# Batch 0's second softmax part summed beside its products, and nine gate blocks of group 0 split into 384 and 128 columns

## The chip, the cores and the metric

The kernel runs on one core of one Trainium2 chip. The metric is the device time of one execution in microseconds. Five runs of the kernel before took 347.96 to 348.55 us, with a median of 348.24 us. The profile is of one execution, which took 348.22 us; its span, from the first to the last recorded instruction, is 346.4 us.

## What is computed

Sliding-window attention with an ALiBi bias, and then a gated feed-forward layer on its output. Batch is 8, heads are 8, the sequence is 576 long, a head has 64 dimensions; the model width is 512 and the hidden width 1536. Inputs and output are fp32.

```python
scores = scale * np.matmul(q, k.transpose(0, 1, 3, 2))
mask = (rel >= 0) & (rel < 128)                    # rel = query - key
scores = np.where(mask, scores + bias[None], -1e9) # bias = -slope[head] * |rel|
attn = np.exp(scores - scores.max(-1, keepdims=True))
attn = attn / (attn.sum(-1, keepdims=True) + 1e-09)
x = np.matmul(attn, v)              # then heads side by side: 4608 rows of 512
g = x @ w_gate                      # 512 -> 1536
gelu = 0.5 * g * (1.0 + erf(g / sqrt(2)))
out = (gelu * (x @ w_val)) @ w_out  # 1536 -> 512
```

## The kernel before

**Layout.** `xT` holds the attention's result transposed: 128 partitions by four pairs of heads by tokens, in bf16. One pair of heads fills 128 partitions, 64 for each head. The feed-forward layer works on groups of 512 tokens, g = 0 to 8. A batch has 576 tokens, so groups and batches don't coincide. For a group and each of twelve blocks f of 128 hidden columns, `gate_val` makes two chains of four matmuls (over the four pairs), one with `w_gate` and one with `w_val`, each into its own PSUM bank. ScalarE takes the gelu of the first, VectorE multiplies it with the second and writes the tile `hT` (lines 512, 518, 519). `out_part` later multiplies `hT` with `w_out` (line 548).

**PSUM.** There is one pool of eight banks of 128 by 512 fp32. A bank is handed on when the last reader of its earlier content is done. So a matmul that begins a new bank can wait for a gelu, a copy or a multiply of some steps ago.

**Attention of batch 0.** It is done before the loop over groups, in two parts of the queries: 0 to 383 and 384 to 575 (`PARTS`). Keys come in blocks of 64, and each meets the 192 queries that its window can reach; scores lie transposed, keys on partitions, so that `P` (exponentials, bf16) can be used as the moving operand. For queries 0 to 383, `biases0` puts the bias into the bank by a matmul and `scores0` adds the scores; the exponential (line 193) reads the bank. For the rest, `scores0_rest` makes the exponentials without bias, and VectorE multiplies them with `emask` (line 196, `mask`), which holds the bias and the window.

**Sums and inverse of the second part.** `sums4` makes the sums over keys as 32-row results (64 matmuls, line 347), VectorE inverts them (line 352), `spread4` copies each inverse to 64 rows by 16 fp32 matmuls (line 361), ScalarE and VectorE move these to `recip` (line 371), `values` makes the products with v (line 429, 40 matmuls) and VectorE multiplies product and inverse into `xT` (line 484). In `products` the upper and lower 64 rows of the array work at the same time, in 64 by 64 tiles; where the two halves of the keys meet in one bank, a relay through SyncE's queue (line 322) orders them.

Batch 1 has another form, `values_and_sums`: the sums are made by matmuls with a tile of ones (`ones64`) that is 64 columns wide, so that every sum comes out 64 times, on the rows where it is used. They go through `products` with the products with v, and ScalarE inverts them by a logarithm and an exponential.

**Order.** The schedule is manual: each engine executes its instructions in the order in which the code names them. Around the change it is, on TensorE: the scores, first part's sums and products; the spread (`spread_first`, whose multiplies at line 498 write `xT` for tokens 0 to 383); three pairs of heads of `scores0_rest`; block 0 of group 0 in two halves of 192 columns, block 1 on 384; the sums of the second part; block 2 on 384; spread and products of the second part; blocks 0 to 2 on the last 128 columns; blocks 3 to 11 on all 512, with the transposes of batch 1 (line 144) behind blocks 9 and 11. A list `waiting` passed to `gate_val` puts off the gelu and the multiply of a block, so that ScalarE and VectorE meet them later in their order.

**Transfers.** GpSimd issues the loads (lines 102, 127, 134, 735) in the order of the code, eight in flight at most: each waits for the landing of the one eight places before it. The gate weights come in pieces of 128 to 256 hidden columns; columns 512 to 1279 are issued between 14.44 and 18.10 us.

Of the kernel before, what the change touches and what calls it, by code (L numbers as in the profile page):

```python
# [7 lines left out]
FP32 = mybir.dt.float32  # L8
BF16 = mybir.dt.bfloat16
AF = mybir.ActivationFunctionType  # L10
ALU = mybir.AluOpType
# [3 lines left out]
PARTS = (((0, 384), (384, 576)), ((0, 256), (256, 576)))  # L15
# [12 lines left out]
def kernel(  # L28
# [10 lines left out]
    nc = tc.nc  # L39
    B, H, S, D = q.shape  # L40
# [3 lines left out]
    NF = DFF // 128  # L44
# [18 lines left out]
        return psum.tile([128, 512], FP32, name="ps")  # L63


    def keep_busy(ps, n):
        for _ in range(n):
            nc.tensor.matmul(out=ps[:, 0:64], lhsT=zeros, rhs=zeros[:, 0:64], start=True, stop=True)

    wg = consts.tile([128, 4, DFF], BF16, name="wg")  # L70
    wv = consts.tile([128, 4, DFF], BF16, name="wv")
# [1 line left out]
    xT = consts.tile([128, 4, RING], BF16, name="xT")  # L73
# [99 lines left out]
    T = consts.tile([128, H, S], BF16, name="T")  # L173
# [21 lines left out]
    def mask(dst, m):  # L195
        nc.vector.tensor_tensor(out=dst, in0=dst, in1=m, op=ALU.mult)  # L196
# [26 lines left out]
    def biases0(cs, idle=0):  # L223
        pss = []
        for c in cs:
            ps = [bank(), bank()]
            pss.append(ps)
            keep_busy(ps[0], idle)
            for i in (0, 1):
                nc.tensor.matmul(  # L230
                    out=ps[i][:, 0:384].rearrange("p (n x) -> p n x", n=2),
                    lhsT=slopes[:, 2 * c + i, :], rhs=dist.unsqueeze(1).to_broadcast((128, 2, 192)),
                    start=True, stop=False, skip_group_check=True)
                nc.tensor.matmul(
                    out=ps[i][:, 384:512], lhsT=slopes[:, 2 * c + i, :], rhs=dist[:, 0:128],
                    start=False, stop=False, skip_group_check=True)
        return pss

    def scores0(cs, pss):
        for c, ps in zip(cs, pss):  # L240
            for n in range(3):
                for x in (0, 1):
                    q0 = 128 * n + 64 * x
                    w = min(192, 384 - q0)
                    for i in (0, 1):
                        score(0, c, i, 2 * n + x, q0, w,
                              ps[i][64 * x:64 * x + 64, 192 * n:192 * n + w], False)
        for c, ps in zip(cs, pss):
            for i in (0, 1):
                exp(prob(0)[:, c, i, 0:512], ps[i])  # L250
# [238 lines left out]
    def products_first(copies):  # L489
        n = PARTS[0][0][1]  # L490
        for c, ps in enumerate(products(0, [(c, c, 0, n, 0) for c in range(4)])):
            copies[c](out=recip[0][:, c, 0:n], in_=ps[:, 0:n])

    def spread_first():
        _, w = shape(0, 0)
        for g, ps in enumerate(spread4_banks(0, 0)):
            c, x = 2 * (g % 2), g // 2
            nc.vector.tensor_tensor(
                out=xT[:, c:c + 2, w * x:w * x + w], in0=recip[0][:, c:c + 2, w * x:w * x + w],
                in1=ps[:, 0:2 * w].rearrange("p (c x) -> p c x", c=2), op=ALU.mult)  # L500
# [3 lines left out]
    def gate_val(g, f, lo=0, hi=512, later=None):  # L504
        if g not in hid:
            hid[g] = h_pool.tile([128, NF, 512], BF16, name="hT")
        t0 = 512 * g % RING
        n = hi - lo
        pg, pv = bank()[:, 0:n], bank()[:, 0:n]
        for w, ps in ((wg, pg), (wv, pv)):  # L510
            for c in range(4):
                nc.tensor.matmul(  # L512
                    out=ps, lhsT=w[:, c, 128 * f:128 * (f + 1)],
                    rhs=xT[:, c, t0 + lo:t0 + hi], start=(c == 0), stop=(c == 3))

        def act():
            gl = g_pool.tile([128, 512], BF16, name="gelu")
            nc.scalar.activation(out=gl[:, 0:n], in_=pg, func=AF.Gelu)  # L518
            nc.vector.tensor_tensor(out=hid[g][:, f, lo:hi], in0=pv, in1=gl[:, 0:n],  # L519
                                    op=ALU.mult)  # L520

        if later is None:
            act()
        else:
            later.append(act)
# [165 lines left out]
    for t in kT + qT:  # L691
        nc.vector.memset(t[:, :, 576:640], 0.0)
    scores0((1,), biases0((1,)))
    ps0 = biases0((2,))
    second(1, (dve, dve))
    scores0((2, 3), ps0 + biases0((3,)))
    decays(5, 6)
    dve(out=pairs1.rearrange("p x (h d) -> p x h d", d=64),
        in_=vb[1].rearrange("p j x -> p (j x)")[:, 0:1536].rearrange(
# [3 lines left out]
            rest(w, cs, dve)  # L703
    row(0)
    masks = []
    nc.scalar.copy(out=sel8, in_=sel0[:, 0:8:2].unsqueeze(2).to_broadcast((128, 4, 64)))
    sums4(0, 0, lambda: scores0_rest((0,), masks))
    products_first((act, act, act, act))
# [3 lines left out]
    spread_first()  # L712
    decays(6, 8)
    scores0_rest((1,), masks)
    for args in masks:
        mask(*args)
    masks.clear()
    scores0_rest((2, 3), masks)
    masks_of_last_blocks(4, 8)
    for args in masks:  # L720
        mask(*args)
    masks.clear()
    for lo in (0, 192):
        gate_val(0, 0, lo, lo + 192)
    waiting = []
    gate_val(0, 1, 0, 384, waiting)
    sums4(0, 1)
    waiting.pop()()
    gate_val(0, 2, 0, 384)
    spread4(0, 1, (act, dve, act, dve))  # L730
    values(0, 1)
    for f in range(3):
        gate_val(0, f, 384, 512)
    for n in range(2):
        nc.gpsimd.dma_start(
# [25 lines left out]
        return [("table",), 4, ("pv", b - 1), ("s", b, 0, (0,)), 4, ("s", b, 0, (1, 2, 3)), 4,  # L761
                ("s", b, 1, range(4)), ("add", b, 0), ("add", b, 1), 4]

    def flush():
        for args in masks:
            mask(*args)
        masks.clear()


    def exp_table():  # L770
        nc.scalar.preload_act_table_set("natural_log_exp_and_others")
# [4 lines left out]
    for g in range(NG):  # L776
        if 1 <= g < B - 2:
            transposes_dma(3 if g == 1 else g + 2)
        if g == 1:

            nc.gpsimd.tensor_copy(out=mark, in_=qT[1][0:1, 0, 512:514])
            load_qk(4)
            load_v(3)
        for f in range(3 if g == 0 else 0, NF):
            gate_val(g, f)
            if g == 0 and f in (9, 11):
                for c in (0, 1) if f == 9 else (2, 3):
                    for w in (0, 1):
                        transpose(1, w, c, (act, dve)[w])
            if g == 2 and f == 0:  # L790
                add(3, 1)
            if 2 <= g < B - 1:
                if f == (4 if g == 2 else 2):
                    sums4(g + 1, 0)
                    sums4(g + 1, 1)
                if f == (6 if g == 2 else 3):
                    gather(g + 1)
                if f == (8 if g == 2 else 5):
                    spread_dma(g + 1)
                if f == 9 and g + 2 < B:  # L800

                    nc.gpsimd.tensor_copy(out=mark, in_=hid[g][0:1, f, 0:2])  # L802
                    if g + 3 < B:
                        load_qk(g + 3)
                    load_v(g + 2)
        if g == 0:
            nc.gpsimd.memset(Ps[0][:, :, 0:64], 0.0)
            for t in (qs[1], ks[1]):
                nc.gpsimd.memset(t[64:128, 4, :], 0.0)
        for item in steps(g):  # L810
            if isinstance(item, int):
                out_part(g, item)
            else:
                RUN[item[0]](*item[1:])
        store()
        if g == 0:

            nc.gpsimd.tensor_copy(out=mark, in_=kT[0][0:1, 0, 512:514])
            load_qk(3)
            load_v(2)  # L820
# [30 lines left out]
```

## Time and profile before

| what | value |
|---|---|
| median of five runs | 348.24 us (347.96 to 348.55) |
| profiled execution | 348.22 us, span 346.4 us |
| TensorE busy | 338.5 us, 98% of the span |
| VectorE, ScalarE, GpSimd busy | 186.4, 171.6, 107.4 us |
| gate and value matmuls (line 512) | 112.1 and 111.6 us busy |
| output matmuls (line 548) | 96.1 us busy |
| granted TensorE clock | full speed in every slice |

How to read it: a matmul's recorded duration includes the filling of the pipe, and neighbours overlap. The time that a row of matmuls takes is the distance between starts. A remark in square brackets is the idle time of the engine before the row, with what ended it; "issue" is time in which the engine waited for nothing that the profile shows. PE is TensorE, PEld its weight loads, ACT ScalarE, DVE VectorE, POOL GpSimd, SP SyncE. A number such as L512 is a line of the kernel, and a helper's line stands for all its uses. Names in `out<-in` are the program's tiles (`ps` is a PSUM bank, `P` the exponentials, `vb` v, `r` the inverted sums, `rb` the tile `recip`).

### The profile page before, as it was taken

The page shows a single profiled execution, that of the slowest core. Times are in us where ns is not written, and L with a number is a line of the kernel's source. Part 1 is how long each engine was busy: PE and PEld are TensorE (multiplying, and loading weights), DVE is VectorE, ACT ScalarE, POOL GpSimd, SP SyncE. Part 2 cuts the span into 40 slices and gives each one's busy share as a digit, 9 for nine tenths or more (in the row PEclk, how much of TensorE's full clock was granted, in tenths as well). Part 3 has the DMA queues.
Part 4 walks back from the last instruction along what each step waited for, and adds up shares of the span by engine and source line. Part 5 has one row for each costly group of instructions (what it writes and reads, how often), then busy time and mean ns, then how long its engine had stood idle before and what let it go on. Part 6 is the DMA issues. An engine that isn't in the chain of part 4 may idle for free.

```text
span 346.4 us, 8167 instructions
## 1 busy us (share of the span) xinstructions
PE 338.5 (98%) x3368; PEld 170.2 (49%) x3368; DVE 186.4 (54%) x333; ACT 171.6 (50%) x328; POOL 107.4 (31%) x143
## 2 busy tenths in 40 slices
PE   8889999999999999999999999999999999999995
PEld 6665555444544454445544454445444544444443
DVE  6884464434669646953796378635873413303320
ACT  6763488636896337533663447344733133224322
POOL 8865671770590085007700590040000000000000
PEclk9999999999999999999999999999999999999999
DMA  9999999999899399979996899589106120020002
GB/s 174 172 197 190 205 156 172 130 186 169 94 183 194 70 186 182 181 157 94 180 178 147 91 178 189 109 128 112 62 12 128 39 85 0 3 91 30 2 30 91
DMA packets 149705, 43.09 MB, mean 124 GB/s; under 512 B 134532, under 2 KB 142628, under 8 KB 149668
## 3 DMA queue, kind: packets, MB, share of 16 engines
q0 software_dynamic: 108480, 18.49, 70.0%
q1 hardware_dynamic: 37744, 17.70, 21.0%
q10 hardware_dynamic: 3444, 6.38, 8.9%
q8 instruction: 26, 0.43, 0.5%
q14 instruction: 11, 0.09, 0.1%
HBM read 43.65 MB, written 9.53 MB: 154 GB/s over the span
## 4 chain that ended last, share of the span: by engine, by line
PE 88%; ACT 7%; DVE 2%; issue 1%; DMA 1%; ACTq 0%; SPq 0%; DVEq 0%
PE ps L512 54%; PE ps L548 23%; PE ps L429 5%; ACT P L193 5%; PE ps L188 3%; PE ps L347 1%; ACT osb L553 1%; DMA wo<-in_q_dram 1%; DVE osb L553 1%; PE ps L144 1%; PE ps L566 1%; PE ps L361 1%; ACT rb L456 0%; ACT rb L457 0%; PE ps L230 0%
## 5 line engine op out<-in xcount | busy, mean ns | idle before, releaser
L519 DVE TENSOR_TENSOR hT<-ps,gelu 128x512 bf16<-128x512 f32 (+3 forms) x112 | 73.8, 668 | 101.6 <-PE ps L512 91.9
L518 ACT ACTIVATE gelu<-ps 128x512 bf16<-128x512 f32 (+3 forms) x112 | 64.3, 582 | 106.8 <-PE ps L512 98.7
L512 PE MATMUL ps<-xT,wg 128*128 128x512 bf16 (+3 forms) x448 | 112.1, 372 | 0.5 <-DVE xT L484 0.3
L512 PE MATMUL ps<-xT,wv 128*128 128x512 bf16 (+3 forms) x448 | 111.6, 371 | 0.0
L548 PE MATMUL ps<-wo,hT 128*128 128x512 bf16 x420 | 96.1, 380 | 0.0
L512 PEld LDWEIGHTS <-wv 128*128 128x128 bf16 x448 | 43.4, 98 | 50.2 <-issue 0.2
L512 PEld LDWEIGHTS <-wg 128*128 128x128 bf16 x448 | 42.8, 98 | 49.7 <-issue 0.8
L193 ACT ACTIVATE P<-ps 128x384 bf16<-128x384 f32 (+2 forms) x128 | 56.2, 549 | 20.1 <-PE ps L188 19.8
L548 PEld LDWEIGHTS <-hT 128*128 128x128 bf16 x420 | 39.0, 98 | 46.6
L196 DVE TENSOR_TENSOR P<-P,emask 128x768 bf16<-128x768 bf16 (+1 forms) x60 | 34.8, 588 | 20.4 <-ACT P L193 19.6
L102 POOL DMA_DIRECT2D vb<-in_v_dram x40 | 34.0, 903 | 5.2 <-DMA ks<-in_k_dram 1.8
L553 ACT COPY osb<-ps 128x512 f32<-128x512 f32 x25 | 14.7, 589 | 34.2 <-PE ps L548 34.1
L802 POOL COPY mark<-hT 1x2 bf16<-1x2 bf16 x4 | 0.7, 174 | 86.3 <-DVE hT L519 86.3
L102 POOL DMA_DIRECT2D qs<-in_q_dram x30 | 25.2, 860 | 6.5 <-DMA wo<-in_moe_w_out_dram 4.4
L102 POOL DMA_DIRECT2D ks<-in_k_dram x30 | 25.4, 902 | 0.0
L188 PE MATMUL ps<-qT,kT 64*64 64x192 bf16 (+2 forms) x656 | 20.1, 237 | 1.5 <-issue 0.7
L188 PEld LDWEIGHTS <-kT 64*64 64x64 bf16 x656 | 13.2, 107 | 12.1 <-issue 10.0
L484 DVE TENSOR_TENSOR xT<-ps,rb 128x512 bf16<-128x512 f32 (+3 forms) x33 | 15.5, 536 | 6.4 <-PE ps L429 6.4
L429 PE MATMUL ps<-P,vb 64*64 64x192 bf16 (+2 forms) x736 | 17.5, 222 | 0.2
L429 PEld LDWEIGHTS <-vb 64*64 64x64 bf16 x736 | 14.5, 107 | 4.2 <-issue 2.7
L278 DVE TENSOR_TENSOR T<-P 64x1024 bf16<-64x1024 bf16 (+1 forms) x20 | 15.0, 751 | 0.4
L352 DVE RECIPROCAL r<-ps 128x128 f32<-128x128 f32 (+3 forms) x12 | 11.9, 1026 | 0.2 <-PE ps L347 0.2
(82 smaller groups left out, 156.0 us busy)
## 6 DMA issues: line engine op xcount, KB each, us to landing
out_dram<-osb SPq DMA_DIRECT2D x35, 256.0 KB
rb<-rd ACTq DMA_DIRECT2D x10, 576.0 KB
vb<-in_v_dram POOLq DMA_DIRECT2D x32, 128.0 KB, 6.8
qs<-in_q_dram POOLq DMA_DIRECT2D x24, 128.0 KB, 5.2
ks<-in_k_dram POOLq DMA_DIRECT2D x24, 128.0 KB, 6.0
wo<-in_moe_w_out_dram POOLq DMA_DIRECT2D x2, 768.0 KB, 14.7
wg<-in_moe_w_gate_dram POOLq DMA_DIRECT2D x5, 256.0 KB, 8.1
wv<-in_moe_w_val_dram POOLq DMA_DIRECT2D x5, 256.0 KB, 8.7
```

Source lines behind the costliest of these rows:

```text
L102: nc.gpsimd.dma_start(out=t[0:n, j, :].rearrange("p (h d) -> p h d", h=H), in_=src[b][:, 128 * j:128 * j + n, :].rearrange("h p d -> p h d"))
L188: nc.tensor.matmul(out=out, lhsT=keys(b, c, m)[half, :], rhs=qT[b % 2][half, c, q0:q0 + n], start=first, stop=True, skip_group_check=not f ...
L193: nc.scalar.activation(out=dst, in_=src, func=AF.Exp, scale=0.125)
L196: nc.vector.tensor_tensor(out=dst, in0=dst, in1=m, op=ALU.mult)
L278: nc.vector.tensor_tensor(out=to[half, :, 2 * n0 + x:2 * n1 + x - 1:2], in0=P[half, :, 3 * n0:3 * n1 - 2:3], in1=P[half, :, 3 * n0 + 1:3 * ...
L429: mm = nc.tensor.matmul(out=out, lhsT=lhsT, rhs=prob(b)[half, c, i, col:col + q1 - q0], start=all(t[2] != u for t in todo[:n]), stop=True, ...
L484: nc.vector.tensor_tensor(out=xT[:, c, at:at + e - a], in0=src, in1=recip[b][:, c, a:e], op=ALU.mult)
L512: nc.tensor.matmul(out=ps, lhsT=w[:, c, 128 * f:128 * (f + 1)], rhs=xT[:, c, t0 + lo:t0 + hi], start=(c == 0), stop=(c == 3))
L518: nc.scalar.activation(out=gl[:, 0:n], in_=pg, func=AF.Gelu)
L519: nc.vector.tensor_tensor(out=hid[g][:, f, lo:hi], in0=pv, in1=gl[:, 0:n], op=ALU.mult)
L548: nc.tensor.matmul(out=acc[g], lhsT=hid[g][:, f, 128 * t:128 * (t + 1)], rhs=wo[:, f, :], start=(f == 0), stop=(f == NF - 1))
L553: (nc.vector.tensor_copy if g < B - 2 and t in by_dve.get(g, (0, 2)) else nc.scalar.copy)(out=osb, in_=acc[g])
```

## The change

Four things change, all in group 0 and batch 0.

- The transposes of k for the pairs 2 and 3 (`second(1, ...)`) come before the bias matmuls of pair 2, and pairs 2 and 3 are done one after the other.
- Block 0's first half (tokens 0 to 191) runs between the scores of pair 1 and those of pairs 2 and 3; both its halves put off gelu and multiply until ScalarE is past the exponentials.
- The second part's sums are made by `products` in the form of batch 1, with `ones64`, in one sequence with the products with v (`products_rest`): 20 and 40 matmuls. VectorE inverts the four banks' halves in four reciprocals of 192 columns, spread between the multiplies of blocks 1 to 5 (`inverse_rest`). Their results are put in the unused tile `T`, read as fp32. ScalarE copies the products from PSUM to `recip` in two copies, and one multiply of VectorE (`scale_rest`) writes `xT`. `sums4`, `spread4` and `values` of that part fall away.
- Blocks 2 to 8 run on columns 0 to 383 first, and then blocks 0 to 8 on the last 128. The loop over groups begins at block 9 for group 0.

`keep_busy` has a width as an argument that nothing here uses, and `flush` moves up in the file.

```diff
+    lo0 = PARTS[0][1][0]
+    inverse = T.rearrange("p h x -> p (h x)").bitcast(FP32)[:, 0:4 * (S - lo0)].rearrange(
+        "p (c x) -> p c x", c=4)
+
+    def products_rest():
+        w = S - lo0
+        pss = products(0, [(n, slice(2 * n, 2 * n + 2), lo0, S, 0) for n in (0, 1)] + [
+            (2 + c // 2, c, lo0, S, w * (c % 2)) for c in range(4)])
+        for n in (0, 1):
+            nc.scalar.copy(out=recip[0][:, 2 * n:2 * n + 2, lo0:S],
+                           in_=pss[2 + n][:, 0:2 * w].rearrange("p (c x) -> p c x", c=2))
+        return pss
+
+    def inverse_rest(c, pss):
+        w = S - lo0
+        nc.vector.reciprocal(inverse[:, c, :], pss[c // 2][:, w * (c % 2):w * (c % 2) + w])
+
+    def scale_rest():
+        nc.vector.tensor_tensor(out=xT[:, :, lo0:S], in0=recip[0][:, :, lo0:S], in1=inverse, op=ALU.mult)
...
     scores0((1,), biases0((1,)))
-    ps0 = biases0((2,))
     second(1, (dve, dve))
-    scores0((2, 3), ps0 + biases0((3,)))
+    for c in (2, 3):
+        scores0((c,), biases0((c,)))
...
     scores0_rest((1,), masks)
-    for args in masks:
-        mask(*args)
-    masks.clear()
+    flush()
+    waiting = []
+    gate_val(0, 0, 0, 192, waiting)
     scores0_rest((2, 3), masks)
     masks_of_last_blocks(4, 8)
-    for args in masks:
-        mask(*args)
-    masks.clear()
-    for lo in (0, 192):
-        gate_val(0, 0, lo, lo + 192)
-    waiting = []
+    flush()
+    gate_val(0, 0, 192, 384, waiting)
+    for later in waiting:
+        later()
+    waiting.clear()
     gate_val(0, 1, 0, 384, waiting)
-    sums4(0, 1)
+    pss = products_rest()
+    inverse_rest(0, pss)
     waiting.pop()()
-    gate_val(0, 2, 0, 384)
-    spread4(0, 1, (act, dve, act, dve))
-    values(0, 1)
-    for f in range(3):
+    for f in range(2, 9):
+        gate_val(0, f, 0, 384)
+        if f < 5:
+            inverse_rest(f - 1, pss)
+        if f == 5:
+            scale_rest()
+    for f in range(9):
         gate_val(0, f, 384, 512)
...
-        for f in range(3 if g == 0 else 0, NF):
+        for f in range(9 if g == 0 else 0, NF):
```

More of the change, by code (lines that the diff above doesn't have):

```diff
@@ L63, in bank, with keep_busy @@
         return psum.tile([128, 512], FP32, name="ps")
-    def keep_busy(ps, n):
+    def keep_busy(ps, n, w=64):
         for _ in range(n):
-            nc.tensor.matmul(out=ps[:, 0:64], lhsT=zeros, rhs=zeros[:, 0:64], start=True, stop=True)
+            nc.tensor.matmul(out=ps[:, 0:w], lhsT=zeros, rhs=zeros[:, 0:w], start=True, stop=True)
     wg = consts.tile([128, 4, DFF], BF16, name="wg")
@@ L705, with flush @@
     masks = []
+    def flush():
+        for args in masks:
+            mask(*args)
+        masks.clear()
     nc.scalar.copy(out=sel8, in_=sel0[:, 0:8:2].unsqueeze(2).to_broadcast((128, 4, 64)))
@@ L762, in steps @@
                 ("s", b, 1, range(4)), ("add", b, 0), ("add", b, 1), 4]
[L764 to L767, printed above, removed]
     def exp_table():
```

## The prediction

> **What bounds the kernel now.** I read the page's first part, then the chain that ended last, then the order of time of each engine between 8 and 46 us, the only stretch that the edit touches.
>
> ```profile
> PE 338.5 (98%) x3368; PEld 170.2 (49%) x3368; DVE 186.4 (54%) x333; ACT 171.6 (50%) x328; POOL 107.4 (31%) x143
> ...
> PE 88%; ACT 7%; DVE 2%; issue 1%; DMA 1%; ACTq 0%; SPq 0%; DVEq 0%
> ```
>
> TensorE is busy for 98% of the span and is 88% of the chain. A microsecond taken off its queue, in work or in waiting, is a microsecond off the end, as long as nothing else becomes late. From 28 us on it hardly waits, so all is won or lost before that.
>
> ```profile
> 18.25 0.47 PE L188 MATMUL ps<-qT,kT 64*64 64x192 bf16 x17 [0.75 <-issue]
> 18.65 0.50 PE L512 MATMUL ps<-xT,wg 128*128 128x192 bf16 x4
> ...
> 19.98 0.81 PE L512 MATMUL ps<-xT,wg 128*128 128x384 bf16 x4
> 20.63 0.81 PE L512 MATMUL ps<-xT,wv 128*128 128x384 bf16 x4
> 21.37 1.03 PE L347 MATMUL ps<-P,ones 64*32 64x64 bf16 x64
> 22.34 0.82 PE L512 MATMUL ps<-xT,wg 128*128 128x384 bf16 x4
> 23.00 0.81 PE L512 MATMUL ps<-xT,wv 128*128 128x384 bf16 x4
> 23.74 0.93 PE L361 MATMUL ps<-r,sel 32*128 32x96 f32 x16
> 24.60 0.96 PE L429 MATMUL ps<-P,vb 64*64 64x64 bf16 x40
> 25.91 1.01 PE L512 MATMUL ps<-xT,wg 128*128 128x128 bf16 x4 [0.34 <-DVE xT L484]
> 26.75 0.38 PE L512 MATMUL ps<-xT,wv 128*128 128x128 bf16 x4
> 26.97 0.39 PE L512 MATMUL ps<-xT,wg 128*128 128x128 bf16 x4
> ...
> 27.87 1.03 PE L512 MATMUL ps<-xT,wg 128*128 128x512 bf16 x4
> ```
>
> This is TensorE in order of time (start, duration, matmuls). Durations overlap, so I take costs from one start to the next. Four matmuls cost 0.65 us on 384 columns (19.98 to 20.63), 0.22 us on 128 (26.75 to 26.97), 0.864 us on 512 (27.87 to 28.73): 163, 56 and 216 ns each. The second part of batch 0 is seen whole: 64 sums (L347), 16 spread matmuls in fp32 (L361), 40 products (L429), then a hole, since the gates of the last 128 columns wait for xT piece by piece.
>
> ```profile
> 11.14 2.06 ACT L193 ACTIVATE P<-ps 128x512 bf16<-128x512 f32 x4 [0.98 <-PE ps L188]
> ...
> 18.58 1.64 ACT L193 ACTIVATE P<-ps 128x384 bf16<-128x384 f32 x4 [0.19 <-PE ps L188]
> 20.23 1.28 ACT L518 ACT_TABLE_LOAD   x1
> 21.53 0.94 ACT L518 ACTIVATE gelu<-ps 128x192 bf16<-128x192 f32 x3
> ```
>
> ScalarE: at 11.14 it had stood idle 0.98 us for the scores of heads 4 and 5. From 18.58 it is full: exponentials, table, gelus.
>
> ```profile
> 14.56 1.36 DVE L352 RECIPROCAL r<-ps 128x192 f32<-128x192 f32 x1 [0.21 <-PE ps L347]
> ...
> 17.99 1.01 DVE L498 TENSOR_TENSOR xT<-rb,ps 128x384 bf16<-128x384 f32 x2
> ...
> 20.45 1.03 DVE L196 TENSOR_TENSOR P<-P,emask 128x768 bf16<-128x768 bf16 x2
> ```
>
> VectorE: one reciprocal of 192 columns, 1.36 us; the xT products of the first part, which end at 17.60, 18.06, 18.53 and 19.00; the last masks, done at 21.48.
>
> **The change, part by part.** Times are on the clock of before; part 1's shift comes on top.
>
> 1. *Transposes of k moved ahead of a bias (8.9 to 13.2 us).* The 12 transposes start right behind the scores that begin at 8.62, at 8.95, not at 9.51 (their k landed at 8.55: issued at 2.25, 6.3 us to landing). They take 0.47 us. VectorE's copy of pair 2 then waits for its memsets, done at 9.59, and starts at 9.60, not 10.07. Scores and the exponentials at 11.14 follow 0.47 earlier, and the copy at L698 at 10.62, not 11.01 (its transfer landed at 10.4). As ScalarE's four exponentials end at 12.7 instead of 13.2, the sums behind them, the reciprocal, the spread and xT all move. Value: -0.45. If k lands late or a copy is held: 0; a loss is excluded, as the moved work is the same.
>
> 2. *First gate block split around the scores.* Its first half (8 matmuls on 192 columns, 0.083 us each) now needs only the first two xT products. Two go at 17.72; six wait for 18.06 + 0.12 (18.53 to 18.65 is that delay in the trace) and end at 18.68. 24 scores at 0.024 us: 19.26; 8 gates: 19.93. Before: 19.98. Value: -0.05. The 0.75 us gap put down to issue falls at the twentieth matmul from 16.93. There TensorE is now held by xT until past 18.25, so it costs nothing; were it to come again elsewhere, +0.75.
> The price is on ScalarE: scores 4 and 5 end at 18.97, 0.2 us later their exponentials start (19.17, not 18.58), 1.64 us, table 1.28 us: the two gelus end at 22.44 and 22.66, some 0.6 us later than before.
>
> 3. *Sums beside the products.* Removed from f1's end (21.28) to f3's start (27.87), 6.59 us: all but f2 (1.30) and three blocks of 128 (1.34), so 3.95 us: sums, spread, products 2.7 and waits 1.2. Added: 60 matmuls (20 sums, 40 products). In the built program they wait for the last mask (21.5), run ten sums, then wait for the banks of the two halves of block 0, so for both gelus: 22.72. The 46 left at 0.022 us are 1.03. That per-matmul cost is the second part of batch 1, which has the same shape (102 matmuls, 57.46 to 59.71); the first part there gives 0.032, so +0.45 as the high end. With 0.1 for the change of tiling f2 starts at 23.85: 2.62 us from f1's end at 21.23, against 3.95. Value: -1.33. Behind these waits stand f2 and all gates.
>
> 4. *384, then 128 columns.* Six more blocks are split: 6 x 8 x (163 + 56 - 216 ns) = +0.13 us. f2 to f8 run from 23.85 to 32.98, the nine narrow blocks take 72 x 56 ns = 4.0 us.
> Here a rule speaks against the change. The Trainium skill ("TensorE: Matmul & The Clock Gate", section "Back-to-back issue gap") gives 81 ns as the sustained spacing of 128-column matmuls that each load weights, and 56 ns only for the isolated gap. By it the narrow blocks cost 72 x 25 ns = 1.8 us more and the sum turns to about +0.1. The row here has weights loaded for each, and 20 of them from 26.75 to 27.87 keep 56 ns; the same rule's 131 ns for 512 columns is 216 here. I take the row.
>
> 5. *VectorE in place of the spread.* Four reciprocals of 192 columns (1.36 each) and one scaling, among the multiplies of f1 to f5 (0.53), under f2 to f8's 9.1 us of TensorE. No row shows a scaling of 768 columns from two fp32 tiles in SBUF. The rows of 192, 384 and 512 columns (346, 548, 690 ns) give 140 + 1.075 per column: 0.97 us; the Trainium skill ("VectorE: DVE Perf Modes", section "Mode 2×_2P — use both read ports for one tensor") holds fp32 tensor_tensor at 1×, at 0.96 GHz 0.80 us plus a fixed part, an estimate. I take 0.97. Queue: first reciprocal at 23.5, two copies on ScalarE, f1's gelu to 25.1, multiplies of f1 and f2 to 26.4, then three reciprocals, three multiplies, scaling: done near 32.7. TensorE asks for it at 32.98. Cover: 0.3 us; each tenth that a reciprocal is longer takes 0.4 of it. Banks and gelu buffers come free over 0.4 us ahead.
>
> 6. *Transfers.* Weights are wanted earlier: f8 at 31.7, not 36.5.
>
> ```profile
> wv<-in_moe_w_val_dram POOLq DMA_DIRECT2D x1, 256.0 KB, 10.0
> ```
>
> That is its transfer, issued at 18.10, landed at 28.1. GpSimd's queue is unchanged but for its memset of T, which now waits for the scaling; it ran at 36.68, so nothing moves. The transfer for f10 landed at 37.06, wanted near 40. All stay hidden.
>
> Sum: -0.45 - 0.05 - 1.33 + 0.13 = -1.70 us. The profiled execution took 348.22 us (span 346.4 and 1.8 around it): 346.5. The median of the runs is 348.24, so the two can be compared.
>
> **Rivals.**
> - *Part 1 gives nothing* (k's landing at 8.55 or the memsets hold it): 346.95. For it: 0.05 us between landing and need.
> - *VectorE becomes the bound*: at 1.6 us a reciprocal the scaling ends 1.0 later, 0.7 past its cover: 347.2; with the sums at 0.032 us a matmul 347.7. Against: the row at L352 has the same shape.
> - *Narrow blocks at 81 ns*, at the nine blocks: 348.3, slower than before by 0.1. It decides from 79 ns; from 90 ns it is measurably slower. Against: the 20 matmuls above.
> - *The gain is lost later*, since a transfer holds batch 1 (its v landed at 49.2, first used at 53.4): 348.2. Against: TensorE's list of waits names nothing over 0.1 us behind 27 us.
> - *The gelus hold less than I think* (TensorE finds its banks at once): another 0.7 off, 345.8.
>
> **How the numbers follow.** Forecast 0.55 (own range 346.1 to 347.0), part 1 empty 0.13, VectorE 0.14, narrow blocks 0.06, lost later 0.07, fewer waits 0.05. Leaving out the narrow blocks, the loss and the worst of VectorE gives 345.8 to 347.6. 0.2% (0.70 us) is about what a measurement can tell from no change. Faster: 0.55 + 0.13 + 0.12 + 0.05 = 0.85. Of the rest 0.10 stays within the bound and 0.05 is slower.
>
> **What would show it.** Part 1: four exponentials from about 10.7. Part 2: TensorE held near 17.9, not at "issue". Part 3: L361 with 16 matmuls, not 32; in the second part a wait for a gelu of 0.5 to 0.9 us, then 46 matmuls in about 1 us. Part 4: 128-column matmuls at 56 ns over nine blocks, and f9 1.7 us earlier than 38.23. Part 5: the scaling ends before the first narrow block. I am wrong if TensorE waits for xT there, if narrow blocks pass 60 ns, or if f9 comes early and the end doesn't.

## The result, and the profile after

The changed kernel takes 346.72 us (median of 22 runs, 346.19 to 348.43); the kernel before takes 348.26 us beside it (43 runs). The ratio is 0.9943, with a 95% interval of 0.9929 to 0.9957: faster by 1.5 us. The profiled execution took 347.24 us (span 345.4), half a microsecond more than the median, and what was late in it is seen below. In many runs, of the kernel before too, TensorE's granted clock fell to half for some microseconds (a mean clock of about 0.99 over the run), and the medians of such runs lie 0.6 to 2.3 us above those of the others; so where it matters I give beside the median of all runs, as "at full clock", that of the runs with a mean clock of at least 0.998: for the changed kernel 21 of 23 (with the profiled one), at 346.71.

The first part of the page of the changed kernel, and its chain that ended last:

```profile
PE 336.7 (97%) x3356; PEld 171.5 (50%) x3356; DVE 189.8 (55%) x337; ACT 172.8 (50%) x334; POOL 107.5 (31%) x143
...
PE 86%; ACT 7%; DMA 2%; DVE 2%; issue 1%; POOL 1%; POOLq 0%; ACTq 0%; DVEq 0%
```

TensorE lost 1.8 us of work (338.5 before), though the span fell by 1.0 only: DMA has gone from 1% to 2% of the chain. TensorE in order of time shows where (start, duration, matmuls, and in brackets the idle time before and what ended it):

```profile
10.18 0.41 PE L188 MATMUL ps<-qT,kT 64*64 64x192 bf16 x12 [0.21 <-DVE kT L152]
...
12.54 0.60 PE L682 MATMUL ps<-ident,wo 64*128 64x64 bf16 x24 [1.06 <-DVE wo L720]
...
16.52 0.93 PE L361 MATMUL ps<-r,sel 32*128 32x192 f32 x16 [0.40 <-ACT rb L492]
17.38 0.36 PE L188 MATMUL ps<-qT,kT 64*64 64x128 bf16 x12
18.21 0.70 PE L534 MATMUL ps<-xT,wg 128*128 128x192 bf16 x4 [0.47 <-ACT emask L639]
...
20.30 0.81 PE L534 MATMUL ps<-xT,wg 128*128 128x384 bf16 x4
20.95 0.81 PE L534 MATMUL ps<-xT,wv 128*128 128x384 bf16 x4
21.70 0.70 PE L429 MATMUL ps<-P,ones 64*64 64x128 bf16 x10
22.91 0.65 PE L429 MATMUL ps<-P,vb 64*64 64x128 bf16 x17 [0.51 <-ACT gelu L540]
...
24.12 0.82 PE L534 MATMUL ps<-xT,wg 128*128 128x384 bf16 x4
```

The kernel before had, on TensorE and then on VectorE:

```profile
12.01 0.60 PE L660 MATMUL ps<-ident,wo 64*128 64x64 bf16 x24 [0.45 <-DVE wo L698]
...
16.93 0.57 PE L188 MATMUL ps<-qT,kT 64*64 64x128 bf16 x19
```

```profile
11.01 0.94 DVE L698 COPY wo<-vb 128x1536 bf16<-128x1536 bf16 x1
```

From above: the scores of pair 2 come early (part 1), but the transposes at 12.54 wait 1.06 us and are 0.53 *later* than before. So the scores of pair 1's second part start at 17.38 instead of 16.93. The row at 18.21, the first half of block 0, waits 0.47 us; it names ScalarE's `emask`, which ended at 18.09, but the first tile of xT that it needs was done at 18.06 (VectorE's L520), and the traces of six variants put the same wait down to xT. From there on the change wins: f1 ends at 21.60, ten sums run, TensorE waits for the gelus, and f2 starts at 24.12. The blocks that follow, up to f9:

```profile
32.58 0.81 PE L534 MATMUL ps<-xT,wv 128*128 128x384 bf16 x4
33.23 0.39 PE L534 MATMUL ps<-xT,wg 128*128 128x128 bf16 x4
...
37.25 1.03 PE L534 MATMUL ps<-xT,wg 128*128 128x512 bf16 x4
```

Seven blocks on 384 columns take 9.11 us, 163 ns a matmul; nine on 128 take 4.02 us, 72 matmuls at 55.8 ns. f9 starts at 37.25, not 38.23. From f9 to the end both spans have 308.2 us, so nothing is given back later.

ScalarE and VectorE of the same execution:

```profile
10.64 2.06 ACT L193 ACTIVATE P<-ps 128x512 bf16<-128x512 f32 x4 [0.53 <-PE ps L188]
...
19.58 1.64 ACT L193 ACTIVATE P<-ps 128x384 bf16<-128x384 f32 x4 [0.73 <-PE ps L188]
21.23 1.28 ACT L540 ACT_TABLE_LOAD   x1
22.53 0.55 ACT L540 ACTIVATE gelu<-ps 128x192 bf16<-128x192 f32 x2
```

```profile
11.53 0.95 DVE L720 COPY wo<-vb 128x1536 bf16<-128x1536 bf16 x1 [0.94 <-DMA vb<-in_k_dram]
...
23.88 1.36 DVE L511 RECIPROCAL T<-ps 128x192 f32<-128x192 f32 x1 [0.37 <-PE ps L429]
...
31.40 0.94 DVE L514 TENSOR_TENSOR xT<-rb,T 128x768 bf16<-128x768 f32 x1
```

The four exponentials start at 10.64, not 11.14, as part 1 meant. But VectorE's copy from vb stood idle for 0.94 us until k's rows had landed, and ran at 11.53. The scaling ended at 32.34, and the narrow blocks wanted it at 33.23.

In this execution the steps add up to: +0.45 at 17.38, -0.13 from there to the end of block 0 (part 2: f1 starts 0.32 later, not 0.45), -1.43 from f1's end to f2 (2.52 us against 3.95), +0.13 for the narrow blocks: -0.98, which is the shift of f9.

### The profile page after: what moved, and what is told of

Its sections match the earlier page's. It is cut to its first block, busy times and chain, and to the rows that moved or that the text cites. A ratio compares the mean times of both kernels' runs of the same rounds, so it can differ in the third digit from the quotient of the medians.

```text
span 345.4 us, 8164 instructions
## 1 busy us (share of the span) xinstructions
PE 336.7 (97%) x3356; PEld 171.5 (50%) x3356; DVE 189.8 (55%) x337; ACT 172.8 (50%) x334; POOL 107.5 (31%) x143
## 4 chain that ended last, share of the span: by engine, by line
PE 86%; ACT 7%; DMA 2%; DVE 2%; issue 1%; POOL 1%; POOLq 0%; ACTq 0%; DVEq 0%
PE ps L534 54%; PE ps L570 23%; PE ps L429 5%; ACT P L193 4%; DMA vb<-in_k_dram 2%; PE ps L188 2%; PE ps L347 1%; ACT osb L575 1%; DVE osb L575 1%; PE ps L588 1%; PE ps L144 1%; ACT rb L456 0%; ACT rb L457 0%; ACT L540 0%; PE ps L361 0%
## 5 line engine op out<-in xcount | busy, mean ns | idle before, releaser
L540 ACT ACTIVATE gelu<-ps 128x512 bf16<-128x512 f32 (+3 forms) x118 | 65.3, 561 | 103.2 <-PE ps L534 97.1
L534 PEld LDWEIGHTS <-wv 128*128 128x128 bf16 x472 | 45.0, 98 | 48.8
L534 PEld LDWEIGHTS <-wg 128*128 128x128 bf16 x472 | 44.3, 98 | 48.6 <-issue 0.9
L196 DVE TENSOR_TENSOR P<-P,emask 128x768 bf16<-128x768 bf16 (+1 forms) x60 | 34.8, 588 | 20.5 <-ACT P L193 19.6
L484 DVE TENSOR_TENSOR xT<-ps,rb 128x512 bf16<-128x512 f32 (+3 forms) x29 | 14.3, 562 | 6.3 <-PE ps L429 6.3
L352 DVE RECIPROCAL r<-ps 128x128 f32<-128x128 f32 (+2 forms) x11 | 11.1, 1050 | 0.1
```

Source lines behind the costliest of these rows:

```text
L484: nc.vector.tensor_tensor(out=xT[:, c, at:at + e - a], in0=src, in1=recip[b][:, c, a:e], op=ALU.mult)
L534: nc.tensor.matmul(out=ps, lhsT=w[:, c, 128 * f:128 * (f + 1)], rhs=xT[:, c, t0 + lo:t0 + hi], start=(c == 0), stop=(c == 3))
```

## The experiments

My theory was the forecast: each part gives what its step says. Its rival after this trace: the transfer into vb holds part 1 in any case. The first four kernels ask that; the next four take the other parts one by one; the last four follow what these showed. The groups ran on different chips, each beside the kernel before.

### Part 1: alone, undone, and with no transfer to wait for

The kernel before with part 1 alone:

```diff
-    ps0 = biases0((2,))
     second(1, (dve, dve))
-    scores0((2, 3), ps0 + biases0((3,)))
+    for c in (2, 3):
+        scores0((c,), biases0((c,)))
```

> The kernel before, with part 1 alone (the transposes of k ahead of the two biases). Step 1 of the forecast: 0.45 us less, 347.8 us, the four exponentials from about 10.7 and the 24 transposes (ps from wo) from about 11.6 instead of 12.01. Rival, read from the trace of after: the copy into wo waits for the transfer of k's runs into vb, which lands about when the copy was due before; then the exponentials move to 10.7 but the transposes stay at 12.0 or later, and the median stays at 348.1 to 348.3.

Measured: 348.38 us (14 runs), before 348.52 beside it, ratio 1.0005 (0.9978 to 1.0031); at full clock 348.24 and 348.37. Part 1 alone gives about a tenth of a microsecond or nothing. The interval of the ratio, -0.8 to +1.1 us, could not tell 0.45 from nothing; the runs at full clock just can (-0.13, with a 95% interval of -0.37 to 0.14 when these runs are resampled). The changed kernel with the same lines put back:

```diff
+    ps0 = biases0((2,))
     second(1, (dve, dve))
-    for c in (2, 3):
-        scores0((c,), biases0((c,)))
+    scores0((2, 3), ps0 + biases0((3,)))
```

> The changed kernel with part 1 undone. Step 1 of the forecast: 0.45 us more than the changed kernel's median of 346.72, so 347.15. Rival (the transfer holds the copy in any case): 346.7 to 346.85.

Measured: 346.97 (22 runs), at full clock 346.76 against the changed kernel's 346.71. That is 0.05 more at full clock (-0.15 to 0.41 by the same resampling) and 0.25 over all runs. By the ratios to the kernel before, 0.9955 (0.9941 to 0.9969) and 0.9943, it is 0.4, but their intervals overlap. At full clock both experiments leave out step 1's 0.45, though the second does so narrowly, and the traces show where it goes. The transfer is a part of the reason, and not the whole of it. This is VectorE, and then TensorE, with part 1 alone:

```profile
10.30 0.95 DVE L698 COPY wo<-vb 128x1536 bf16<-128x1536 bf16 x1 [0.40 <-DMA vb<-in_k_dram]
```

```profile
11.31 0.60 PE L660 MATMUL ps<-ident,wo 64*128 64x64 bf16 x24 [0.52 <-DVE wo L698]
...
16.22 0.57 PE L188 MATMUL ps<-qT,kT 64*64 64x128 bf16 x19
18.54 0.47 PE L188 MATMUL ps<-qT,kT 64*64 64x192 bf16 x17 [1.75 <-issue]
```

In this execution TensorE's scores of pair 1 ran at 7.87, before at 8.62, so all had a head start of 0.75 us; 0.66 of it was there at the first scores (5.84, before 6.50), ahead of the place of the edit. Part 1 added its 0.45 to that up to the exponentials, and the copy, held by the transfer for 0.40, gave it back: the scores of 16.22 are 0.71 ahead of before's 16.93, the head start alone. Then comes what I had not looked for. TensorE stopped at the twentieth of these matmuls, at the same place as before, for 1.75 us instead of 0.75, and resumed at 18.54, before at 18.25. The gap put down to "issue" took the whole head start; I conclude that it would have taken part 1's gain with it.

The two other kernels take the transfer's landing out, by letting the copy read rows that landed long before. The scores of batch 0's columns from 384 on are then made from other rows, by the same instructions:

```diff
     dve(out=pairs1.rearrange("p x (h d) -> p x h d", d=64),
-        in_=vb[1].rearrange("p j x -> p (j x)")[:, 0:1536].rearrange(
+        in_=qs[0].rearrange("p j x -> p (j x)")[:, 0:1536].rearrange(
```

In the changed kernel:

> The changed kernel, but the copy into wo reads from qs, which has landed by 8 us, in place of vb: batch 0's scores of the columns from 384 on are made from the wrong rows, with the same instructions and the same transfers. If the transfer into vb is what held part 1's gain: the copy starts at about 10.6, the transposes from 11.6, f9 near 36.3, and the median falls by 0.3 to 0.5 from 346.72, to 346.2 to 346.4, with a narrower spread of the runs (the profiled run within 0.2 of the median). If the transfer held it in the profiled run alone: median 346.65 to 346.75.

In the kernel before:

> The kernel before with the same edit (the copy into wo reads qs; batch 0's scores of the columns from 384 on are made from the wrong rows). In its trace the copy ran at 11.01 when VectorE came to it, with the transfer landed at 10.4: if that is its usual state, nothing changes: 348.15 to 348.3. If the transfer holds before's copy too in most runs: 347.9 or less. Under either, runs above 349.5 become rare if they are late landings of this transfer, and stay if they are something else.

Measured: 346.99 (9 runs; at full clock 346.96), and 348.66 (14 runs; 348.48 at full clock, before 348.37). Nothing was gained by either; at full clock the first was 0.25 slower than the changed kernel. This is TensorE of the first of the two:

```profile
16.32 0.36 PE L188 MATMUL ps<-qT,kT 64*64 64x128 bf16 x12
17.27 0.69 PE L534 MATMUL ps<-xT,wg 128*128 128x192 bf16 x4 [0.59 <-DVE xT L520]
...
19.11 0.33 PE L534 MATMUL ps<-xT,wv 128*128 128x192 bf16 x2 [0.97 <-issue]
```

Here part 1 gave all that step 1 promised: its copy ran at 10.40 without a wait, and from the scores of pair 1 (8.46) to those of 16.32 are 7.86 us, in the kernel before 8.31. And yet the third of wv's matmuls waited 0.97 us at the gap, to 19.11, with part 2 in place. The transfer takes part 1's gain in some executions (the copy waited for it 0.15 to 0.94 us in five of the eight traces that have both part 1 and this wait), and where it doesn't, the gap does.

### What the gap is

The page's list of DMA queues has two of kind "instruction". The larger, q8, has 26 packets, 0.43 MB, so about 16 KB each; the transfer view by windows shows when each starts. With part 1 alone, 16.00 to 17.00 us:

```profile
q0 software_dynamic: 458, 0.18, 146.6%
q8 instruction: 1, 0.02, 6.8%
```

One such packet starts in that stretch, among 458 of the loads, and takes about 1.1 us (6.8% of the time of sixteen DMA engines). In the kernel before the same packet starts at 15.89. Set against TensorE's gaps:

| kernel | TensorE ready | packet starts | TensorE resumes | resume - packet |
|---|---|---|---|---|
| before | 17.50 | 15.89 | 18.25 | 2.36 |
| part 1 alone | 16.79 | 16.06 | 18.54 | 2.48 |
| before, no transfer | 16.80 | 15.82 | 18.27 | 2.45 |
| split alone (below) | 17.43 | 15.87 | 18.23 | 2.36 |
| changed, no transfer | 18.14 | 16.79 | 19.11 | 2.32 |
| changed, no part 2 (below) | 16.79 | 15.74 | 17.99 | 2.25 |
| changed, f2 first (below) | 18.07 | 15.93 | 18.33 | 2.40 |
| changed, short cover (below) | 18.28 | 16.12 | 18.55 | 2.43 |

"Ready" is the end of the matmuls before the gap, and varies by 1.5 us; "resumes" follows the packet, at 2.25 to 2.48 us. The packet takes about 1 us of that; what fills the rest the profile does not show. In the changed kernel's own trace the packet started at 15.87, so by the same distance its instructions were there at about 18.2, and TensorE, late by the transfer and held until 18.21, did not meet the gap.

In three of these traces (part 1 alone, f2 first, short cover) there is a first gap of the same sort, of 0.17 to 0.30 us, at the last of the first 32 sums (L347). Between it and the second gap lie, with f2 first, 1 + 12 + 32 + 48 + 16 + 12 + 4 + 2 = 127 matmuls, each with a weight load: 254 instructions, and a few waits. The Trainium skill ("Runtime: NRT & Kernel Launch", section "Instruction fetch mechanics") says that an engine's instruction memory is refilled in blocks of 16 KiB, 256 instructions, through a DMA queue of its own; packet size and spacing agree, and roughly the number: the changed kernel's 3356 matmuls and as many weight loads are 6712 instructions, 26.2 blocks, which is why I take q8 for TensorE's queue. It also calls the crossing of a block "mostly hidden": here it was not. It cost 0.17 to 1.75 us, in a stretch in which all DMA engines were busy with loads and TensorE ran short instructions.

To test it, I made TensorE's stream shorter without changing its work in time: the warm-up at the start as 32 matmuls on 128 columns, not 64 on 64.

```diff
-    keep_busy(held[0], 64)
+    keep_busy(held[0], 32, 128)
```

> The changed kernel with the warm-up at the start made of 32 matmuls on 128 columns in place of 64 on 64: the same TensorE time, 32 matmuls (64 instructions with their weight loads) fewer in TensorE's stream. In the traces so far the gap put down to issue stands at the same place of the stream (two gaps 127 matmuls apart, 256 instructions with the waits between), and it ends 2.3 to 2.45 us after the second 16 KB packet of the instruction queue starts, whenever TensorE arrived. If the block of instructions arrives by its own time: the gap's place moves 32 matmuls later, behind the scores of pairs 2 and 3, where TensorE comes after 19 us, no gap is left before 20 us, and the median falls from 346.71 by the 0.26 to 0.97 us of the gaps in the traces of its variants, less what the wait for xT takes over: 346.2 to 346.5. If the block is fetched when TensorE asks for it, the gap moves along and keeps its size: 346.7.

Measured: 348.84 (22 runs), 347.50 in its four runs at full clock: slower than the changed kernel, so my expectation was wrong. But the trace shows where the gap belongs:

```profile
12.78 0.46 PE L347 MATMUL ps<-P,ones 64*32 64x128 bf16 x19
14.96 0.47 PE L347 MATMUL ps<-P,ones 64*32 64x64 bf16 x13 [1.71 <-issue]
```

The first gap now stands 32 matmuls further down: from the last of the first 32 sums, past 12 scores, to the twentieth of the second 32. The first packet started at 12.79 instead of 10.18 to 10.45 (the eleven kernels with the old warm-up; 12.2 and 12.3 in the two other runs with the short one), and TensorE resumed 2.17 us later. So the gap belongs to a place in the stream, a block's boundary, and the packet is not on a fixed timetable: with the stream 64 instructions shorter, TensorE reaches the boundary later, and the packet came later too. The same with part 1 undone:

> The same with part 1 undone. If the instruction block was what swallowed part 1's gain, part 1 is worth its 0.45 us once the block is out of the way: 0.3 to 0.45 above the run with part 1 and the short warm-up, with scores (1) starting near 16.9 to 17.2 here and near 16.3 there. If part 1 is empty for another reason, the two agree within 0.1.

Measured: 348.90 (22 runs; six at full clock, 347.69). That doesn't tell part 1's worth with the block out of the way, as the block wasn't out of the way:

```profile
14.70 0.47 PE L347 MATMUL ps<-P,ones 64*32 64x64 bf16 x13 [1.04 <-issue]
```

TensorE was ready at 13.66 and resumed at 14.70; with part 1 it was ready 0.41 earlier, at 13.25, and resumed at 14.96. It came earlier and waited longer, by 0.67.

What makes a packet start when it does is not settled. In all fourteen traces the second packet of the stretch starts 5.4 to 6.4 us after the first, however early TensorE was; a chain in which a block is asked for after the one before has come would look like that. I have no run that shows it.

### Part 4 alone

The kernel before, with its own sums, spread and products, but f3 to f8 on 384 columns and then nine blocks on 128:

```diff
     values(0, 1)
-    for f in range(3):
+    for f in range(3, 9):
+        gate_val(0, f, 0, 384)
+    for f in range(9):
         gate_val(0, f, 384, 512)
...
-        for f in range(3 if g == 0 else 0, NF):
+        for f in range(9 if g == 0 else 0, NF):
```

> The kernel before, with part 4 alone: f3 to f8 on 384 columns behind the old sums, spread and products, then nine blocks on 128. Step 4: six more blocks split cost +0.13; the wait of 0.34 us for xT ahead of the first narrow block, which the blocks on 384 now cover, goes, and the narrow blocks all run at 56 ns: 348.0 to 348.1. By the 81 ns rule: 72 x 25 ns more, 349.9.

Measured: 347.76 (21 runs), before 348.49, ratio 0.9964 (0.9947 to 0.9980); at full clock 347.56 and 348.27. That is 0.7 us faster, where I expected 0.15 to 0.25. The trace:

```profile
24.57 0.96 PE L429 MATMUL ps<-P,vb 64*64 64x64 bf16 x40
25.47 0.82 PE L512 MATMUL ps<-xT,wg 128*128 128x384 bf16 x4
...
33.28 0.39 PE L512 MATMUL ps<-xT,wg 128*128 128x128 bf16 x4
...
37.30 1.03 PE L512 MATMUL ps<-xT,wg 128*128 128x512 bf16 x4
```

A gate starts at 25.47, 0.90 after the products began. In the kernel before the first narrow block began at 25.91 and its second half at 26.75, since its matmuls waited piece by piece for xT: from 25.50, 0.90 behind the start of its products, the first 8 narrow matmuls took until 26.97: 1.47 us, for 0.45 of work. So the hole behind the products was 1.02 us, not the 0.34 that the bracket names ahead of it. It is gone, less 0.13 for the split: -0.89, and f9 is at 37.30, against 38.23, 0.93 earlier. The 72 narrow matmuls take 4.02 us, 55.8 ns each, here too, and not the 81 ns that step 4 of the forecast quotes.

### The cover of VectorE's work

The changed kernel with f2 to f5 only ahead of the narrow blocks, and f6 to f11 on 512 columns:

```diff
-    for f in range(2, 9):
+    for f in range(2, 6):
...
-    for f in range(9):
+    for f in range(6):
         gate_val(0, f, 384, 512)
...
-        for f in range(9 if g == 0 else 0, NF):
+        for f in range(6 if g == 0 else 0, NF):
```

> The changed kernel with only f2 to f5 on 384 columns ahead of the narrow blocks (f0 to f5), f6 on at 512. By step 5 the cover is TensorE's work on blocks f2 to f8: without three of them the narrow blocks start at 24.12 + 4 x 1.30 = 29.3 but the scaling ends near 31.9, so TensorE waits about 2.5 us for xT: about 2.4 us slower than the changed kernel, 349.1, and slower than before. If VectorE's chain could be done much earlier than it was: 346.7.

Measured: 350.94 (18 runs), 349.45 at full clock; 2.7 us slower than the changed kernel, and slower than before (ratio 1.0060, 1.0044 to 1.0076). TensorE, and below it VectorE:

```profile
32.05 0.40 PE L534 MATMUL ps<-xT,wg 128*128 128x128 bf16 x4 [2.92 <-DVE xT L514]
```

```profile
23.52 1.36 DVE L511 RECIPROCAL T<-ps 128x192 f32<-128x192 f32 x1 [0.37 <-PE ps L429]
...
31.05 0.95 DVE L514 TENSOR_TENSOR xT<-rb,T 128x768 bf16<-128x768 f32 x1
```

From the first reciprocal to the end of the scaling are 8.5 us, and TensorE waits for them. Part 4's blocks ahead of the narrow ones are what makes part 3's inverse on VectorE free: with three fewer it costs 2.7 us. Part 3 with no block of part 4 was not run.

### Part 2 undone, and f2 ahead of the products

```diff
-    gate_val(0, 0, 0, 192, waiting)
     scores0_rest((2, 3), masks)
     masks_of_last_blocks(4, 8)
     flush()
-    gate_val(0, 0, 192, 384, waiting)
-    for later in waiting:
-        later()
-    waiting.clear()
+    for lo in (0, 192):
+        gate_val(0, 0, lo, lo + 192)
```

> The changed kernel with part 2 undone: scores of pairs 2 and 3 first, then both halves of gate block 0. By the price in step 2, the exponentials start about 0.6 us earlier, so do table load and gelus, and the wait for the gelus inside the products shrinks from 0.5 by up to that: 346.2 us. Rival: the gap of 0.75 us put down to issue, which part 2 hid, comes back behind 17 us: 346.7 to 347.0.

Measured: 346.36 (5 runs, 345.93 to 346.54), ratio to before 0.9934 (0.9910 to 0.9958), against the changed kernel's 0.9943: 0.35 less on the medians, though the intervals overlap. The trace says why, and that both expectations held a part of it:

```profile
17.99 0.47 PE L188 MATMUL ps<-qT,kT 64*64 64x192 bf16 x17 [1.20 <-issue]
...
21.11 0.53 PE L429 MATMUL ps<-P,ones 64*64 64x128 bf16 x10
21.65 0.65 PE L429 MATMUL ps<-P,vb 64*64 64x128 bf16 x17
...
22.85 0.82 PE L534 MATMUL ps<-xT,wg 128*128 128x384 bf16 x4
```

The gap is back, 1.20 us. But the scores of pairs 2 and 3 are out at 18.4, not 19.6, the gelus end at 21.8, and from the end of f1 (21.02) to f2 there are 1.83 us instead of 2.52. What part 2 hid at the gap in the changed kernel's trace it paid at the gelus. With five runs and intervals that overlap, the 0.35 itself is not shown beyond the noise.

f2's 384 columns ahead of the sums, to fill the wait for the gelus:

```diff
+    gate_val(0, 2, 0, 384, waiting)
     pss = products_rest()
     inverse_rest(0, pss)
-    waiting.pop()()
+    for later in waiting:
+        later()
     for f in range(2, 9):
-        gate_val(0, f, 0, 384)
+        if f > 2:
+            gate_val(0, f, 0, 384)
```

> The changed kernel with block f2's 384 columns run ahead of the sums and products. If TensorE's hole between the first ten sums and the seventeen products (about 1.0 us in the trace of after, from 21.95 to 22.91) is only the wait for the banks that the gelus hold, f2 fills it, and f3 starts about 24.4 instead of 25.43: 0.6 to 1.0 us less, 345.7 to 346.1, the lower gain if the scaling (then some 0.3 later, wanted 1.0 earlier) makes the narrow blocks wait. If the products need something else that is late (masks, a mode change), the hole moves behind f2 and the time stays at 346.6 to 346.8.

Measured: 346.41 (5 runs), ratio 0.9937 (0.9913 to 0.9961), 0.3 less:

```profile
21.67 0.81 PE L534 MATMUL ps<-xT,wv 128*128 128x384 bf16 x4
22.41 0.55 PE L429 MATMUL ps<-P,ones 64*64 64x128 bf16 x10
...
24.53 0.81 PE L534 MATMUL ps<-xT,wg 128*128 128x384 bf16 x4 [0.50 <-ACT rb L505]
```

The products now run without a wait, but 0.50 us is lost behind them: f3 needs a bank, and the copies of the products (L505) stand on ScalarE ahead of f1's gelu. So I put the gelus ahead and took the two edits together, with the scaling behind f4's multiply. First, with the short warm-up as well:

```diff
-    gate_val(0, 1, 0, 384, waiting)
+    gate_val(0, 1, 0, 384)
+    gate_val(0, 2, 0, 384)
     pss = products_rest()
     inverse_rest(0, pss)
-    waiting.pop()()
-    for f in range(2, 9):
+    for f in range(3, 9):
         gate_val(0, f, 0, 384)
-        if f < 5:
-            inverse_rest(f - 1, pss)
-        if f == 5:
+        if f == 3:
+            inverse_rest(1, pss)
+        if f == 4:
+            inverse_rest(2, pss)
+            inverse_rest(3, pss)
             scale_rest()
```

> The changed kernel with the short warm-up, without part 2, with f2 ahead of the products, f1's and f2's gelus ahead of the copies of the products, and the scaling behind f4's multiply. From the trace without part 2 (f2 at 22.86, gap of 1.20): without the gap f1 ends about 0.7 earlier, f2 fills what is left of the wait for the gelus, and the products follow: f3 near 22.9 instead of 24.2, f9 near 34.9 to 35.3; 344.6 to 345.3 us. If the gap stays, 345.8 or more; if the scaling becomes late, TensorE waits for xT ahead of the narrow blocks and the time is 345.5 to 346.2.

Measured: 347.66 (13 runs), none at full clock: its trace has the early gap, 1.35 us, and half the clock from 14.2 to 21.0. With the old warm-up:

> The changed kernel with the old warm-up, without part 2, with f2 ahead of the products, f1's and f2's gelus ahead of the copies, the scaling behind f4's multiply. The gap put down to issue stays (16.8 to about 18.0, ended 2.4 us after the instruction packet of 15.8), so f1 ends near 21.1 as in the run without part 2; f2 then fills to 22.4, the products run without a wait for 1.34 us, and f3 starts near 23.75 instead of 24.16: 0.4 less than that run's 346.36, 345.8 to 346.1. If the gains of the run without part 2 and of the run with f2 first are one and the same wait, the two don't add and it stays at 346.3 to 346.45.

Measured: 346.96 (22 runs), 346.08 in its 11 runs at full clock, ratio to before 0.9951 (0.9932 to 0.9970). In its trace the products take 1.26 us and nothing waits; the gap stays (0.80 us, to 18.21), and f3 started at 23.90, where I had 23.75:

```profile
22.64 0.46 PE L429 MATMUL ps<-P,ones 64*64 64x128 bf16 x10
...
23.90 0.82 PE L534 MATMUL ps<-xT,wg 128*128 128x384 bf16 x4
```

At full clock this is the fastest of these kernels, by 0.3 over the two single edits and 0.6 over the changed kernel; over all runs it is not, because half of them have the clock drop. No version here beats the changed kernel beyond the intervals.

## Why the prediction was right, and where it wasn't

The forecast was 346.5, the median is 346.72, within the likeliest case's own range of 346.1 to 347.0. The sum was -1.70 us; the medians give -1.54. That the number held took some luck: step 1's 0.45 did not come, which alone makes 346.97 of the forecast, just inside the range; in the trace steps 2 and 3 gave 0.18 more than forecast, and about 0.1 between that sum (-1.43) and the medians is not accounted for. Of the signs named, "f9 1.7 us earlier" did not show in the profiled execution (0.98); the others did, nearly as written.

- *Step 1, -0.45: failed.* The transposes and exponentials moved as it said (10.64). The step that failed is "the sums behind them, the reciprocal, the spread and xT all move. Value: -0.45". In five of eight traces they didn't in full, as the copy then waited for k's rows in vb, which I had dated from one execution; where they did, TensorE waited longer at the block's boundary. The medians: -0.14 alone, 0.05 to 0.25 when undone. The rival "part 1 gives nothing" is what happened, though not for the reasons that it names (the landing of the k that is transposed, the memsets). The step's own "or a copy is held: 0" covers the first half of it; the gap behind it was not in the forecast for this step.
- *Step 2, -0.05.* In the trace it was -0.13. I had seen the gap of 0.75 and said that it "costs nothing" once TensorE is held by xT. That held in the changed kernel's own trace; in three others with part 2 the gap still cost 0.97, 0.26 and 0.27 us (no transfer, f2 first, short cover). I didn't ask what the gap was, nor apply it to step 1, upstream of the same place: a wait that doesn't end sooner when TensorE comes sooner takes in whatever is gained before it. The price on ScalarE was seen ("some 0.6 us later"), but booked in step 3. Undone, part 2 looks like a loss of about 0.35, on five runs.
- *Step 3, -1.33.* In the trace -1.43: 2.52 us from f1's end to f2, where I had 2.62; the wait ended 1.31 us behind f1, where I had 1.49, and the matmuls after it took 1.21 us to f2, where I had 1.13. Part of that is a slip: behind ten of 60 matmuls 50 are left, as in the trace, not 46. The total was right and its owner wrong. I booked "waits 1.2" among what the sums beside the products remove. The split alone removes 1.02 of them, with the old sums in place. What is left for the merged sums and VectorE's inverse is -1.43 + 1.02 = -0.41, a difference of traces; no run has them without the split.
- *Step 4, +0.13.* The size was exact: 163 and 55.8 ns, and the row was the right choice over the rule of 81 ns, by which the narrow blocks would have cost 1.8 us more. But the split's effect on its own is -0.93 in the trace and -0.7 in the medians.
- *Step 5.* The scaling takes 0.94 us (0.97 forecast), the reciprocals 1.34 to 1.36. It ended at 32.34, 0.9 us ahead of its need, where I had 0.3: the recorded durations overlap, so that a reciprocal and a multiply of f2 to f5 came every 1.67 us, not 1.36 + 0.53. The cover was necessary, as the run with three blocks fewer shows: +2.7.
- *Step 6.* No transfer of weights came late. The one that did in the profiled execution, into vb, I had dated from one trace (10.4); in another it was over 1 us later.

Taken from the traces, the sum reads: part 1 nothing, the split -0.9 (-0.7 on its medians), the merged sums and the inverse -0.4, part 2 some -0.1 at the gap and, as it seems, +0.3 or more at the gelus (which are inside the -0.4).

## What to carry to other kernels

An idle time put down to "issue" needs the question whether it stands at a fixed place in the stream and ends no sooner when the engine comes sooner; if so, a gain ahead of it doesn't arrive behind it. When a hole is removed by an edit of several parts, ask which part alone would remove it: here work to put behind the products was enough, without merging the sums. And the hole is to be measured from the start of one group of matmuls to the next, since the idle time in brackets counts only what lies ahead of the first one.

## What the runs showed of the hardware

- TensorE's instructions arrive in packets of about 16 KB on a queue of their own, and TensorE can run dry between 12 and 19 us of this kernel: gaps of 0.17 to 1.75 us, ended 2.17 to 2.50 us after a packet's start in all fifteen that I found.
- Holes in TensorE's work can be followed by half its clock. With the short warm-up (windows of 2 us; of the last three columns, the first is the granted clock):

```profile
14.00:16.00 2.00, 1.04 (x41) 0.80 (x44) 0.54 (x1) 0.00 (x0) 1.16 (x3) 0.99 2.15 166
16.00:18.00 2.00, 2.00 (x36) 1.77 (x40) 1.70 (x5) 1.37 (x4) 1.98 (x4) 0.50 1.50 194
18.00:20.00 2.00, 1.70 (x24) 0.93 (x21) 1.31 (x3) 1.63 (x5) 1.78 (x3) 0.50 1.44 197
20.00:22.00 2.00, 2.00 (x33) 1.49 (x32) 1.98 (x6) 0.62 (x3) 1.03 (x3) 0.50 1.46 196
22.00:24.00 2.00, 2.00 (x15) 1.48 (x13) 1.12 (x2) 1.98 (x4) 0.98 (x2) 0.80 1.45 195
```

  In all six traces that have it, the last hole before it was 0.97 to 2.92 us long, and it began between 0.3 us before the hole's end and 1.2 after it; that the hole is the cause is inferred from this order. It lasted 3.4 us in four traces and 6.8 in two, which agrees with the window of about 3.4 us in the Trainium skill ("TensorE: Matmul & The Clock Gate", section "Part 1: The HAM clock gate"); the page has the slow clock follow an idle window of that length, and these holes are shorter. It doesn't always come: the hole of 1.75 us with part 1 alone had none in its trace. It was in 2 of the changed kernel's 23 runs, in 11 of 18 with the short cover, and in 18 of 22 with the short warm-up; in the kernel before, in 19 of 46, 11 of 39, 18 of 50 and 8 of 27. So a hole can cost more than its length, and the change gains more on the mean of all runs than on the median: 348.82 to 346.83, 2.0 us; why it meets the drop less is not shown. Why the short warm-up brings it so often is open; its hole of 1.71 us is no longer than that of part 1 alone, but earlier.
